# Moving one chunk's load behind four output stores on a DMA queue

## The chip, the cores and the metric

The kernel runs on one core of a Trainium2 chip. The metric is the device time of one execution in microseconds (us), given as the median of several. TensorE does the matmuls and writes their results to banks of a memory called PSUM; VectorE, ScalarE and GpSimd do the elementwise work, and SyncE issues nearly all DMAs, in program order; "the queue" below is SyncE's. In the profile they are PE (with PEld for its weight loads), DVE, ACT, POOL and SP; a q after the name (SPq, ACTq) is that engine's sequencer, which issues DMAs.

## The reference

```python
# q, k, v: (8 batches, 8 heads, 576 positions, 64)
scores = scale * (q @ k^T)
ret    = scores * Dmat            # gamma_h ** (i - j) for i >= j, else 0
attn   = ret @ v                  # retention, causal, decaying
x      = attn as (4608 tokens, 512)
h      = max(x @ w1, x @ w2, x @ w3)      # w1..w3: 512 x 768
out    = h @ w_out                        # 768 x 512
```

The kernel walks the 4608 tokens in 36 chunks of 128 positions for the attention and in 9 tiles of 512 tokens for the network, four chunks to a tile. While it computes the network of tile t, it prepares the attention of tile t + 1 and loads chunks beyond that.

## The kernel before

These are the parts that matter here, cut. A chunk from number 7 on is loaded in 34 DMAs: 16 small ones for q, 16 for a second copy of k (both laid out so that VectorE can transpose them), one each for k and v. The tiles for q and kx have two buffers, so the load of chunk 10 can't start before chunk 8's has been transposed.

```python
def load_blocks(g, *blocks):
    for n, src in (("q", q), ("kx", k)):
        if 0 in blocks:
            raws[n, g] = raw.tile([P, NP, C // 32, 32], FP32, tag=n, ..., bufs=2)
        for blk in blocks:
            for a in range(4):
                nc.sync.dma_start(raws[n, g][32 * a:32 * a + 32, :, blk, :], src[...])

def load(g):
    if g >= BY_PE and ("q", g) not in raws:
        load_blocks(g, *range(C // 32))
    ...                                     # then k and v, one DMA each (more at a batch border)
```

Tile 0 goes through a plain path, whose last step copies four outputs out of PSUM and stores them. The output tile "osb" has two buffers:

```python
opool = ctx.enter_context(tc.tile_pool(name="opool", bufs=2))
...
def downs_plain(t, h):                      # tile 0
    ps = [(ps_x, ps_y)[m % 2].tile([P, DM], ...) for m in range(4)]
    for fb in range(NF):
        for m, b in enumerate(ps):
            nc.tensor.matmul(b[:], ...)
            if fb == NF - 1:
                osb = opool.tile([P, DM], FP32, tag="osb", name="osb")
                nc.scalar.copy(osb[:], b[:])
                nc.sync.dma_start(out[t * NT + m * P:t * NT + (m + 1) * P, :], osb[:])
        yield
```

Tile 1 starts with 12 plain "up" groups for the feature blocks 2 to 5 (four matmuls, eight records in the trace, each), of which the first three take the PSUM banks ps_x[0], ps_x[1], ps_x[0] in turn, the banks of tile 0's outputs 0 and 2. From then on outputs are made by `downs`, with `total` and `store`, on the same queue and the same "osb" buffers.

The order of work is written by hand, in twelve slots to a tile (cut to tile 0's last slot and the first of the common rule):

```python
if t == 1:
    a, b, c, d = range(CPT, 2 * CPT)        # chunks 4..7, prepared during tile 0
    ...
    at(11, (values, [c, d], [d, d + 1]), (load_blocks, d + 2, 3), (load, d + 2),
       (transposes, d + 1), (load, d + 3))  # d + 3 = chunk 10
    return todo
for n in range(0, CPT, 2):
    a, b, m = CPT * t + n, CPT * t + n + 1, 6 * (n // 2)
    at(m, (keep, a), (transposes, b), (decay_values, b), (load, b + 2))
    ...
```

Of the kernel before, what the change touches and what calls it, by code (L numbers as in the profile page):

```python
# [79 lines left out]
def kernel(  # L80
# [23 lines left out]
    CPT = NT // C  # L104
# [50 lines left out]
    for r in sorted({start_of(g) for g in range(NG)} - {0, None}):  # L155
        m = masks[r] = const.tile([C, C], FP32, name=f"causal{r}")
# [553 lines left out]
    def steps(t):  # L710


        todo = [[] for _ in range(3 * CPT)]

        def at(n, *what):
            for step, *args in what:
                if step is values:
                    if args[0][0] < NG:
                        todo[n].append(partial(values, args[0], [g for g in args[1] if g < NG]))
                elif args[0] < NG:  # L720
                    todo[n].append(partial(soon, partial(step, *args)) if step is load else partial(step, *args))

        if t == 1:
            a, b, c, d = range(CPT, 2 * CPT)
            at(0, (load, b))
            at(1, (scores, a), (state, a), (keep, a))
            at(2, (transposes, b), (decay_values, b), (load, c))
            at(3, (scores, b), (load_blocks, d, 0))
            at(4, (decay_values, c), (load_blocks, d, 1, 2))
            at(5, (values, [a, b], [b, c]), (load_blocks, d, 3), (load, d))  # L730
            at(6, (keep, c), (transposes, c), (load_blocks, d + 1, 0))
            at(7, (transposes, d), (decay_values, d), (load_blocks, d + 1, 1, 2))
            at(8, (scores, c), (scores, d), (load_blocks, d + 1, 3), (load, d + 1))
            at(9, (load_blocks, d + 2, 0, 1))
            at(10, (decay_values, d + 1), (load_blocks, d + 2, 2))
            at(11, (values, [c, d], [d, d + 1]), (load_blocks, d + 2, 3), (load, d + 2),
               (transposes, d + 1), (load, d + 3))
            return todo
        for n in range(0, CPT, 2):
            a, b, m = CPT * t + n, CPT * t + n + 1, 6 * (n // 2)  # L740
            at(m, (keep, a), (transposes, b), (decay_values, b), (load, b + 2))
            at(m + 2, (scores, a), (scores, b))
            at(m + 4, (decay_values, a + 2))
            at(m + 5, (values, [a, b], [b, a + 2]), (transposes, a + 2), (load, a + 4))
        return todo

    for t in range(N // NT):
        work = ffn(t)
        for todo in steps(t + 1):
            for step in todo:  # L750
                step()
            next(work, None)
# [51 lines left out]
```

## Time and profile before

| | before |
|---|---|
| median of 3 runs (range) | 805.69 us (803.97 to 806.81) |
| span of the profiled run | 804.8 us |
| TensorE busy, idle | 774.2, 30.6 us |
| longest single idle stretch of TensorE | 18.02 us, from about 130 to 148 us |
| mean granted clock of TensorE | 0.987 |

TensorE is 96% busy, so read its idle time, not its busy time: one stretch holds well over half of it. The granted clock is the share of full speed that the throttle lets TensorE have; a dip there makes the matmuls themselves longer. The lines for both are in the prediction.

### The profile page before, as it was taken

The page shows a single profiled execution, that of the slowest core. Times are in us where ns is not written, and L with a number is a line of the kernel's source. Part 1 is how long each engine was busy: PE and PEld are TensorE (multiplying, and loading weights), DVE is VectorE, ACT ScalarE, POOL GpSimd, SP SyncE. Part 2 cuts the span into 40 slices and gives each one's busy share as a digit, 9 for nine tenths or more (in the row PEclk, how much of TensorE's full clock was granted, in tenths as well). Part 3 has the DMA queues.
Part 4 walks back from the last instruction along what each step waited for, and adds up shares of the span by engine and source line. Part 5 has one row for each costly group of instructions (what it writes and reads, how often), then busy time and mean ns, then how long its engine had stood idle before and what let it go on. Part 6 is the DMA issues. An engine that isn't in the chain of part 4 may idle for free.

```text
span 804.8 us, 14293 instructions
## 1 busy us (share of the span) xinstructions
PE 774.2 (96%) x4968; PEld 619.6 (77%) x4968; DVE 552.3 (69%) x1224; ACT 316.6 (39%) x782; POOL 100.9 (13%) x124
## 2 busy tenths in 40 slices
PE   8899994699999999999999999999999999999998
PEld 7545451246888888888888888888788888888887
DVE  3897975376868784878387928783869386847672
ACT  3664630002325441544154515450445235524651
POOL 2110000031101120101111111110102010200000
PEclk9999998799999999999999999999999999999999
DMA  9996632410332333233313432334233333201001
GB/s 217 239 213 148 183 69 35 102 34 12 58 90 50 62 58 97 47 63 57 99 25 55 78 81 47 57 60 87 57 58 55 57 91 57 40 14 40 1 0 53
DMA packets 236936, 59.31 MB, mean 74 GB/s; under 512 B 217920, under 2 KB 235584, under 8 KB 236864
## 3 DMA queue, kind: packets, MB, share of 16 engines
q1 hardware_dynamic: 236432, 58.14, 33.5%
q8 instruction: 39, 0.64, 0.3%
q14 instruction: 33, 0.27, 0.1%
q10 hardware_dynamic: 432, 0.27, 0.1%
HBM read 48.89 MB, written 9.44 MB: 72 GB/s over the span
## 4 chain that ended last, share of the span: by engine, by line
PE 89%; DMA 4%; SPq 3%; DVE 3%; issue 1%; ACT 0%; DVEq 0%; ACTq 0%
PE a L579 16%; PE b L579 14%; PE up L600 13%; PE dx L424 9%; PE c L579 7%; PE d L579 5%; PE e L579 4%; PE s L240 4%; PE o L296 4%; PE dz L424 4%; PE dy L424 3%; DMA out_dram<-osb 2%; DVE s L344 2%; PE o L309 2%; PE kv L260 2%; PE down L589 2%
## 5 line engine op out<-in xcount | busy, mean ns | idle before, releaser
L559 DVE TENSOR_TENSOR part<-part 128x256 f32<-128x256 f32 x440 | 197.5, 457 | 61.6 <-ACT part L564 54.6
L564 ACT COPY part<-b 128x256 f32<-128x256 f32 x220 | 81.9, 372 | 151.0 <-PE b L579 137.1
L600 PE MATMUL up<-xT,w 128*128 128x512 f32 x240 | 107.7, 605 | 18.5 <-ACT osb L593 18.0
L564 ACT COPY part<-a 128x256 f32<-128x256 f32 x264 | 98.2, 372 | 53.6 <-PE a L579 43.5
L600 PEld LDWEIGHTS up<-xT,w 128*128 128x128 f32 x240 | 45.6, 193 | 74.4 <-issue 52.1
L579 PE MATMUL b<-s,n 128*128 128x256 f32 x264 | 78.8, 380 | 1.8 <-DVE s L344 1.8
L579 PE MATMUL a<-s,w 128*128 128x256 f32 x264 | 78.5, 379 | 0.0
L211 POOL TENSOR_TENSOR vd<-vraw,gk 128x512 f32<-128x512 f32 x36 | 38.5, 1070 | 228.4 <-DMA vraw<-in_v_dram 177.6
L441 DVE TENSOR_TENSOR osb<-dx,part 128x256 f32<-128x256 f32 x16 | 6.1, 419 | 77.3 <-PE dx L424 70.7
L579 PEld LDWEIGHTS b<-s,n 128*128 128x128 f32 x264 | 49.8, 190 | 9.9 <-ACT part L564 3.3
L579 PEld LDWEIGHTS a<-s,w 128*128 128x128 f32 x264 | 50.2, 190 | 6.8
L579 PE MATMUL c<-xT,w 128*128 128x256 f32 x176 | 54.2, 390 | 0.0
L579 PE MATMUL b<-xT,n 128*128 128x256 f32 x176 | 52.4, 379 | 0.0
L579 PE MATMUL d<-s,w 128*128 128x256 f32 x176 | 52.4, 379 | 0.0
L579 PE MATMUL e<-xT,w 128*128 128x256 f32 x176 | 45.2, 379 | 0.0
L579 PE MATMUL a<-xT,n 128*128 128x256 f32 x176 | 45.2, 379 | 0.0
L424 PE MATMUL dx<-To,H 128*128 128x256 f32 x192 | 44.8, 383 | 0.0
L559 DVE TENSOR_TENSOR h<-part 128x256 f32<-128x256 f32 x88 | 37.4, 425 | 6.3
L424 PEld LDWEIGHTS dx<-To,H 128*128 128x128 f32 x192 | 35.9, 190 | 5.7 <-issue 1.0
L240 PEld LDWEIGHTS s<-qT,kT 64*128 64x128 f32 x576 | 33.7, 188 | 8.1 <-PE b L579 4.0
L402 POOL TENSOR_TENSOR H<-h,H 128x256 f32<-128x256 f32 x24 | 18.2, 759 | 171.9 <-DVE H L401 89.6
L603 DVE TENSOR_TENSOR h<-h,up 128x512 f32<-128x512 f32 x20 | 13.7, 684 | 36.6 <-PE up L600 36.3
(104 smaller groups left out, 1296.1 us busy)
## 6 DMA issues: line engine op xcount, KB each, us to landing
bits<-in_moe_w_dram SPq DMA_DIRECT2D x36, 256.0 KB, 5.1
out_dram<-osb SPq DMA_DIRECT2D x35, 256.0 KB, 2.3
kraw<-in_k_dram SPq DMA_DIRECT2D x32, 256.0 KB, 3.0
vraw<-in_v_dram SPq DMA_DIRECT2D x32, 256.0 KB, 3.4
qraw<-in_q_dram SPq DMA_DIRECT2D x464, 16.0 KB, 1.8
kxraw<-in_k_dram SPq DMA_DIRECT2D x464, 16.0 KB, 1.8
bits<-in_moe_w_out_dram SPq DMA_DIRECT2D x6, 512.0 KB, 5.2
qraw<-in_q_dram SPq DMA_DIRECT2D x6, 256.0 KB, 4.4
```

Source lines behind the costliest of these rows:

```text
L211: nc.gpsimd.tensor_tensor(t[:], raws.pop(("v", g))[:], gk[:].unsqueeze(2).to_broadcast([C, H, D]), op=ALU.mult)
L240: nc.tensor.matmul(s[j][:, p, :], lhsT=kT[r, p, :], rhs=qT[r, p, :], start=True, stop=True)
L260: nc.tensor.matmul(kvs[g][half(h % 2), h // 2, :], lhsT=kr[r:, h, :], rhs=vds[g][r:, h, :], start=True, stop=True)
L296: nc.tensor.matmul(o[n % 2][half(c), m, n // 2, :], lhsT=vds[g][:, h, :], rhs=sts[g][:, h % 2, h // 2, :], start=m == 0 and n < 2, stop=be ...
L309: nc.tensor.matmul(o[n % 2][half(c), m, n // 2, :old], lhsT=states[g][r, h // 2, :], rhs=qks[g]["q"][r, h // 2, :old], start=False, stop=True,
L344: nc.vector.tensor_tensor(dst, a, b, op=ALU.add if sign == "+" else ALU.subtract)
L402: urgent.append(lambda: (pool(s3, a11, a21, op=ALU.subtract), pool(s4, a12, s2, op=ALU.subtract)))
L424: nc.tensor.matmul(out[m], lhsT=hS[n](fp)[:, m * P:(m + 1) * P], rhs=late["T"][n][:, fp, :], start=first and fp == 0 and (m == 0 or last a ...
L559: nc.vector.tensor_tensor(out, a, b, op=op)
L564: nc.scalar.copy(t[:], ps[step[0]][:])
L579: nc.tensor.matmul(ps[chain][:], lhsT=factor(w, fb), rhs=xS[t][x], start=n == 1, stop=ends, skip_group_check=True)
L600: nc.tensor.matmul(ps[:], lhsT=w_sb[i, fb][:, dc * P:(dc + 1) * P], rhs=xT[t][:, dc, :], start=(dc == 0), stop=(dc == NDC - 1))
```

## The change

The intent is to get tile 0's stores out as soon as their data are ready: chunk 10's load leaves the last slot of tile 0 and becomes the first load of the next tile's first slot, which is emitted after the stores.

```diff
             at(11, (values, [c, d], [d, d + 1]), (load_blocks, d + 2, 3), (load, d + 2),
-               (transposes, d + 1), (load, d + 3))
+               (transposes, d + 1))
             return todo
         for n in range(0, CPT, 2):
             a, b, m = CPT * t + n, CPT * t + n + 1, 6 * (n // 2)
-            at(m, (keep, a), (transposes, b), (decay_values, b), (load, b + 2))
+            at(m, (keep, a), (transposes, b), (decay_values, b))
+            if a == 2 * CPT:
+                at(m, (load, a + 2))
+            at(m, (load, b + 2))
```

## The prediction

> **What bounds the kernel now.** I began with the busy shares and the clock strip of the page, then read what stands just before TensorE's one large idle stretch, then followed that stretch back through the waits and the order of ScalarE, of the DMA queue and of VectorE. The page first:
>
> ```profile
> PE 774.2 (96%) x4968; PEld 619.6 (77%) x4968; DVE 552.3 (69%) x1224; ACT 316.6 (39%) x782; POOL 100.9 (13%) x124
> PEclk9999998799999999999999999999999999999999
> L600 PE MATMUL up<-xT,w 128*128 128x512 f32 x240 | 107.7, 605 | 18.5 <-ACT osb L593 18.0
> ```
>
> TensorE is busy for 774.2 of 804.8 us, so all its idle time is 30.6 us, and 18.0 of that stands in one place: ahead of an "up" matmul, released by the copy of a finished output from PSUM (line 593). The clock strip has a dip in the same place, slices 6 and 7 (120.7 to 161.0 us). The waits of 120 to 150 us, TensorE's and ScalarE's, and the queue's of 95 to 200 us, name the links:
>
> ```profile
> PE up L600 <- ACT osb L593: 18.0, 1, 18.0
> ACT osb L593 <- DMA out_dram<-osb: 21.9, 1, 21.9
> SPq L195 <- DVE qT L184: 8.1, 1, 8.1
> ```
>
> TensorE waits for a copy, the copy waits for a store to land (the output tile "osb" has two buffers and tile 0 makes four outputs), and a load on the store's queue waits 8.1 us for a transpose. The timelines of TensorE, ScalarE and the queue put times to this (start us, length us):
>
> ```profile
> 126.52 3.60 PE L600 MATMUL up<-xT,w 128*128 128x512 f32 x8
> 148.13 4.46 PE L600 MATMUL up<-xT,w 128*128 128x512 f32 x5 [18.02 <-ACT osb L593]
> ...
> 124.14 0.59 ACT L593 COPY osb<-down 128x512 f32<-128x512 f32 x1 [11.24 <-PE down L589]
> 125.00 0.58 ACT L593 COPY osb<-down 128x512 f32<-128x512 f32 x1 [0.27 <-PE down L589]
> 147.49 1.23 ACT L593 COPY osb<-down 128x512 f32<-128x512 f32 x2 [21.90 <-DMA out_dram<-osb]
> ...
> 118.92 0.50 SPq L207 DMA_DIRECT2D vraw<-in_v_dram  x1
> 127.61 7.64 SPq L195 DMA_DIRECT2D qraw<-in_q_dram  x16
> 135.29 7.54 SPq L195 DMA_DIRECT2D kxraw<-in_k_dram  x16
> 142.88 0.43 SPq L207 DMA_DIRECT2D kraw<-in_k_dram  x1
> 143.41 0.53 SPq L207 DMA_DIRECT2D vraw<-in_v_dram  x1
> 144.04 5.04 SPq L594 DMA_DIRECT2D out_dram<-osb  x4
> 149.17 7.55 SPq L195 DMA_DIRECT2D qraw<-in_q_dram  x16
> ```
>
> The first output is ready at 124.14 + 0.59 = 124.73. Its store stands in the queue behind the 34 DMAs of chunk 10's load, which can't begin before 127.6, when chunk 8's q buffer has been transposed, and then take 16.4 us to issue. So the store goes out at 144.04, 19.3 us after its data were ready. The third copy follows at 147.49, and only its end (148.1) frees the PSUM bank that the second "up" group of tile 1 wants.
>
> **What the Trainium skill says.** "DMA: Bandwidth & Descriptors", section "Anatomy of one DMA", says that DMA engines wait on no semaphore: a wait is served by the issuing sequencer before it dispatches. So a waiting load holds up the stores queued behind it; the trace agrees (no issue between 119.4 and 127.6 us, though a store was ready at 124.73). The same section gives about 50 ns for a sequencer's dispatch; here an issue takes 7.64 / 16 = 0.48 us, and I use that. "TensorE: Matmul & The Clock Gate", section "Part 1: The HAM clock gate", has the clock at half rate after an idle window of some 3.4 us and back at full rate after about as long a busy one. The stretches view agrees (columns: stretch, length, busy us of TensorE, weight loads, VectorE, ScalarE, GpSimd, granted clock, DMA share, GB/s):
>
> ```profile
> 130.20:148.00 17.80, 0.00 (x0) 0.00 (x0) 0.89 (x3) 0.51 (x1) 0.00 (x0) 0.64 0.38 86
> 148.00:151.00 3.00, 2.87 (x4) 1.32 (x5) 0.00 (x0) 1.15 (x3) 0.00 (x0) 0.50 0.53 186
> 151.00:154.00 3.00, 3.00 (x7) 1.28 (x6) 0.01 (x1) 0.00 (x0) 0.00 (x0) 0.78 0.22 33
> 154.00:157.00 3.00, 3.00 (x8) 1.33 (x7) 2.90 (x7) 0.00 (x0) 0.00 (x0) 1.00 0.24 36
> ```
>
> **The change, part by part.** It adds and removes no instruction. The order of the built programs is the same on TensorE, VectorE, ScalarE and GpSimd; on the DMA queue alone the four stores of tile 0 now stand before chunk 10's 16 + 16 + 1 + 1 DMAs, and chunk 11's load follows as before.
>
> Stores: the first can issue at about 124.8, when the queue is idle. From issue to landing the four stores of before took 2.0 to 3.4 us, median 2.6. It lands between 127.4 and 128.2, the third copy (0.59 us) ends by 128.0 to 128.9, the fourth 0.6 us later. TensorE wants that PSUM bank at 126.52 + 3.60 = 130.12. So the wait of 18.02 us should vanish whole, with 1.2 to 2.1 us to spare. The first "up" group's own copy to h comes after those four on ScalarE, but not before 130.1 in any case.
>
> Clock: after the stall, 24 records of "up" matmuls took 12.62 us (the chain's piece at 148.13). At full clock 16 take 7.06 us (its pieces at 71.76 and 186.95), so 24 take 10.59. Without the idle stretch this 2.03 us goes too.
>
> VectorE is no new limit here: by 131.13 it has done all that it did before the stall, and next needs the second "up" group, at 130.12 + 3.53 = 133.65. In the kernel before it sat idle 22.86 us at this point, and from 154 us on, where the clock is full, TensorE had no pause; that stretch repeats itself earlier.
>
> Sum: 18.02 + 2.03 = 20.05 us, all on the path that sets the end, since the TensorE work after it (96% busy to the end) simply starts that much earlier. 805.69 - 20.05 = 785.64, which I round to 785.7.
>
> **The rivals.** First, the loads come too late, and their wait takes the place of the one removed. The queue is done with the stores at about 130; chunk 10's load then issues until 130 + 16.4 = 146.4 instead of 144.0, while its users move up 20 us. Its last piece, v, lands 3.4 us after its issue (the page's median), so at about 149.3; GpSimd's scaling of it stood at 172.72, so is now due at 152.7. Its transposes stood at 192.83 and are due at 172.8. It holds, by 3.4 us at the closest. Chunk 11's load took 17.0 us (149.17 to 166.12) and ends at about 163.4, its v landing near 166.3. Its scaling stood at 184.70 and is due at 164.65: 1.6 us late. But GpSimd's next instruction stood at 195.16 (now 175.1), and the attention matmuls that read this v stood at 223.8 (now 203.8). So it is absorbed, and the queue, which waited 27.9 us for a transpose before chunk 12's load at 194.15, catches up there. If I am wrong, TensorE idles for some 2 to 5 us in tile 1: 788 to 791.
>
> Second, the store still lands too late, say beyond 4.7 us, or the third copy waits for something else too. Then a pause of one to three microseconds stays, with little or no lost clock if it is below the 3.4 us window: 786.5 to 789. Speaking against it: the store goes out onto nearly idle DMA engines, where in the kernel before it followed two 256 KB loads and still took only 3.4.
>
> Third, the gain is given back later, by waits that were hidden: in tiles 3 to 6 the chain of waits also passes through a store (3.5 to 4.8 us each) ahead of VectorE's sums, and TensorE idles up to 1.5 us per 80 us stretch. Those stand 250 us later, in stages that this change shifts as a whole, since the queue is back in step by 174. I give it 1 us at most.
>
> **Range and chances.** The three runs of before span 2.8 us, so their median is good to about 1 us; the gain itself I hold good to 1.5 us, with a tail upwards from the first two rivals. That makes 784.0 to 788.0. The line of 2% is 805.69 x 0.98 = 789.6, 3.9 us above my figure; only a wait of more than 4 us in tile 1 would cross it. So faster 0.95, within 2% 0.045, slower 0.005, since no instruction was added.
>
> **What would show it.** Right: the first store issues near 124.8 and copies 3 and 4 lie before 130; the "up" group shows no idle of 18 us; the clock strip has no dip in slices 6 and 7; scores follow at 140.7 instead of 160.75; TensorE's idle time in all is about 12.5 us; chunk 10's load issues from about 130 to 146. Wrong: a new idle stretch of TensorE between 130 and 220 released by a DMA, GpSimd or a transpose; or the dip in the clock stays although the idle stretch is gone.

## The result, and the profile after

The changed kernel took 785.23 us (median of 4 runs, 782.70 to 786.94), against 805.92 us for the kernel before (4 runs, 803.97 to 806.81): ratio 0.9744, 95% interval 0.9712 to 0.9776. A ratio is the mean time of one kernel's fast runs over the mean of the other's fast runs of the same rounds, so it is not quite the ratio of the medians quoted.

From the page of the changed kernel, the busy shares, the clock strip and the group of the "up" matmuls:

```profile
PE 770.4 (99%) x4968; PEld 618.3 (79%) x4968; DVE 551.8 (71%) x1224; ACT 316.9 (41%) x782; POOL 100.4 (13%) x124
PEclk9999999999999999999999999999999999999999
L600 PE MATMUL up<-xT,w 128*128 128x512 f32 x240 | 105.4, 595 | 0.5 <-DVE xT L184 0.5
```

Idle before the "up" matmuls fell from 18.5 to 0.5 us, their mean from 605 to 595 ns, and the strip has no dip. TensorE idles 780.9 - 770.4 = 10.5 us in all. Now the timelines of the changed kernel for the same stretch, TensorE, then ScalarE, then the queue:

```profile
124.73 13.90 PE L600 MATMUL up<-xT,w 128*128 128x512 f32 x32
138.56 2.06 PE L240 MATMUL s<-qT,kT 64*128 64x128 f32 x32
...
122.36 0.58 ACT L593 COPY osb<-down 128x512 f32<-128x512 f32 x1 [11.28 <-PE down L589]
123.22 0.59 ACT L593 COPY osb<-down 128x512 f32<-128x512 f32 x1 [0.27 <-PE down L589]
125.15 0.58 ACT L593 COPY osb<-down 128x512 f32<-128x512 f32 x1 [1.35 <-DMA out_dram<-osb]
126.27 0.58 ACT L593 COPY osb<-down 128x512 f32<-128x512 f32 x1 [0.53 <-DMA out_dram<-osb]
...
122.97 4.24 SPq L594 DMA_DIRECT2D out_dram<-osb  x4
127.30 7.52 SPq L195 DMA_DIRECT2D qraw<-in_q_dram  x16
134.87 8.51 SPq L195 DMA_DIRECT2D kxraw<-in_k_dram  x16
```

The first copy ends at 122.94 and its store issues at 122.97. The third copy waits 1.35 us for a store instead of 21.90, and the 32 "up" records that were cut in two run through in one piece.

This trace is 1.79 us ahead of the other one when tile 1 begins (124.73 against 126.52 us); that lead is there at the first "up" matmul of tile 0 already (27.65 against 29.44), before anything that was changed, so it isn't the change's. I therefore compare stretches. From the first "up" matmul of tile 1 to the scores of chunk 8 it is 160.68 - 126.52 = 34.16 us before and 138.56 - 124.73 = 13.83 after: 20.33 us gained there. From those scores to the end it is 644.12 us before and 642.34 after, 1.78 us less (spans are read to 0.1 us, so this is good to about 0.1); most of that is traced below.

### The profile page after: what moved, and what is told of

Same layout as the page of the kernel before. It is cut to its first block, busy times and chain, and to the rows that moved or that the text cites. A ratio compares the mean times of both kernels' runs of the same rounds, so it can differ in the third digit from the quotient of the medians.

```text
span 780.9 us, 14294 instructions
## 1 busy us (share of the span) xinstructions
PE 770.4 (99%) x4968; PEld 618.3 (79%) x4968; DVE 551.8 (71%) x1224; ACT 316.9 (41%) x782; POOL 100.4 (13%) x124
## 4 chain that ended last, share of the span: by engine, by line
PE 95%; DVE 2%; DMA 2%; SPq 0%; issue 0%; POOL 0%; ACT 0%; DVEq 0%; POOLq 0%
PE a L579 17%; PE b L579 14%; PE up L600 13%; PE dx L424 10%; PE c L579 8%; PE d L579 5%; PE e L579 5%; PE dz L424 5%; PE s L240 4%; PE o L296 4%; PE down L589 3%; PE dy L424 3%; PE kv L260 2%; PE o L309 2%; DMA out_dram<-osb 1%; DVE s L344 1%
## 5 line engine op out<-in xcount | busy, mean ns | idle before, releaser
L600 PE MATMUL up<-xT,w 128*128 128x512 f32 x240 | 105.4, 595 | 0.5 <-DVE xT L184 0.5
L472 ACT COPY osb<-dx 128x256 f32<-128x256 f32 x16 | 5.3, 375 | 84.2 <-PE dx L424 72.4
```

Of the source, the lines that this page charges most:

```text
L600: nc.tensor.matmul(ps[:], lhsT=w_sb[i, fb][:, dc * P:(dc + 1) * P], rhs=xT[t][:, dc, :], start=(dc == 0), stop=(dc == NDC - 1))
```

## The experiments

My theory: TensorE waited for a copy, the copy for a store, and the store for the 34 DMAs ahead of it, and the idle stretch then cost 2 us of clock on top. Rivals: that moving the load itself brought the gain; that the wait for chunk 8's transpose, not the issuing, was what held the store; that the slow matmuls after the stall had another cause than the clock.

**Four outputs without a wait.** The kernel before, with the third and fourth output put into two tiles that are unused until tile 1:

```diff
-                    osb = opool.tile([P, DM], FP32, tag="osb", name="osb")
-                    nc.scalar.copy(osb[:], b[:])
+                    if m < 2:
+                        osb = opool.tile([P, DM], FP32, tag="osb", name="osb")[:]
+                    else:
+                        osb = late["S"][m - 1][:, 0:2, :].rearrange("p a f -> p (a f)")
+                    nc.scalar.copy(osb, b[:])
```

(`late["S"]` is also allocated earlier, before tile 0's outputs. Simply giving "osb" four buffers didn't build: the pool allocated after it needed 56 KB a partition and 52.97 were left.)

> The kernel before with its queue order unchanged, but tile 0's third and fourth outputs copied into two other, still unused tiles, so that no copy waits for a store. Theory (TensorE waits for a copy, the copy for a store, the store for 34 DMAs ahead of it on the queue): cutting the chain at the copy is as good as cutting it at the queue. Stores still issue at about 144, yet the third copy comes by 128, the idle stretch of 18 us is gone, time 785.5 (784 to 788). Rival (the gain comes from moving chunk 10's load itself out of 127 to 144 us): nothing gained, 805 to 807.

Measured: 786.35 us (4 runs), ratio 0.9744 (0.9715 to 0.9772). The queue's timeline of this run, and TensorE's:

```profile
128.58 7.63 SPq L195 DMA_DIRECT2D qraw<-in_q_dram  x16
...
145.80 1.00 SPq L597 DMA_DIRECT2D out_dram<-osb  x2
...
127.49 13.90 PE L603 MATMUL up<-xT,w 128*128 128x512 f32 x32
```

The load starts 1.09 us after tile 1's first matmul, exactly as in the kernel before (127.61 - 126.52), and the first store issues at 145.80, as late as ever. Yet TensorE runs through. So the load's time is not the cause; the copies' wait is.

**Tile 0's stores on another queue.** The kernel before, with `nc.scalar.dma_start` for the four stores.

```diff
-                    nc.sync.dma_start(out[t * NT + m * P:t * NT + (m + 1) * P, :], osb[:])
+                    nc.scalar.dma_start(out[t * NT + m * P:t * NT + (m + 1) * P, :], osb[:])
```

> The kernel before with tile 0's four stores issued from ScalarE's queue, the loads untouched. Theory: stores issue at about 125, 126, 128 and 129, third copy by 129, no idle stretch of TensorE, 785.5 (784 to 788), the same as the change although chunk 10's load still issues from 127.6 to 144. Rival (it is the load's time that counts): 805 to 807.

Measured: 785.51 us (4 runs), ratio 0.9742 (0.9700 to 0.9784). The time is as expected, but this run doesn't separate the load's time as cleanly as I meant. The loads didn't stay untouched: chunk 10's issued from 132.10 instead of 127.61, because a load of chunk 9 waited for a store on the other queue (the queue's waits, 110 to 170 us):

```profile
SPq L195 <- DMA out_dram<-osb: 8.8, 1, 8.8
```

In the traces every DMA of these two queues takes one of eight semaphores (the counters that tell of a landing) in turn, and an issue waits until the previous user of its semaphore has landed: the load here issued at 128.67, when the store before it on the same semaphore landed at 128.65. The clean answer is that of the run above.

**Half, and a quarter, of the load ahead.** The changed kernel with 16, then 8, of chunk 10's 34 DMAs put back ahead of the stores. The first of the two edits (the other has block 0 alone ahead):

```diff
-               (transposes, d + 1))
+               (transposes, d + 1), (load_blocks, d + 3, 0, 1))
...
-                at(m, (load, a + 2))
+                at(m, (load_blocks, a + 2, 2, 3), (load, a + 2))
```

> The changed kernel with blocks 0 and 1 of chunk 10 (16 of its 34 DMAs) put back ahead of the stores. Theory (each DMA ahead costs its 0.475 us of issue): first store at 127.6 + 16 x 0.475 = 135.2, lands 2.0 to 2.6 us later, copy done 0.7 after that, TensorE idle 7.9 to 8.4 us from 130.1 (times of the kernel before), lost clock 2.0 to 2.3 us: 10.3 us above the changed kernel, 795.5 (794 to 797.5). Rival (the wait for chunk 8's transpose is what holds the store, the issues hardly count): within 2 us of the run with 8 ahead, whichever level both take.

> The changed kernel with block 0 alone of chunk 10 (8 of its 34 DMAs) put back ahead of the stores. Theory: first store at 127.6 + 8 x 0.475 = 131.4, copy done at 134.1 to 134.7, TensorE idle 4.0 to 4.6 us, lost clock 0 to 2.3 us as the idle stretch is only just longer than a clock window: 785.2 + 4.3 + 1.2 = 790.7 (789 to 792.5). Rival (all or nothing with the wait): the same as with 16 ahead.

Measured: 796.95 us with 16 ahead (4 runs; ratio 0.9876, 0.9843 to 0.9909) and 794.40 us with 8 ahead (4 runs; 0.9845, 0.9806 to 0.9885). The first is in its range; the second is 1.9 us above its own. The medians are 2.55 us apart and the intervals overlap, so the times alone don't exclude the rival's "within 2 us". TensorE's timelines do, 16 ahead first:

```profile
138.37 12.48 PE L600 MATMUL up<-xT,w 128*128 128x512 f32 x24 [8.03 <-ACT osb L593]
```
```profile
137.76 13.50 PE L600 MATMUL up<-xT,w 128*128 128x512 f32 x24 [4.45 <-ACT osb L593]
```

The stalls are 8.03 and 4.45 us, as worked out (7.9 to 8.4 and 4.0 to 4.6): they follow the number of DMAs ahead, with 18.02 for all 34. So the issuing counts, and the rival falls. What I had mis-sized, by this trace, is the clock. The 24 records after the stall take 10.57 us at full clock (next run), so they lost 1.91 us after a stall of 8.03 and 2.93 us after one of only 4.45, more than after 18.02 us (12.62 - 10.57 = 2.05). The stretches view of the run with 8 ahead (columns as in the prediction) shows the dip:

```profile
134.00:138.00 4.00, 0.24 (x1) 0.24 (x2) 0.33 (x1) 0.76 (x2) 0.00 (x0) 0.86 0.45 148
138.00:142.00 4.00, 4.00 (x5) 1.61 (x6) 0.00 (x0) 0.90 (x2) 0.00 (x0) 0.50 0.47 151
142.00:146.00 4.00, 4.00 (x9) 1.67 (x8) 1.46 (x4) 0.00 (x0) 0.00 (x0) 0.79 0.22 33
```

The clock was halved 0.88 us before work came back, and stayed low for the first 5.95 us of it: the same view, cut finer, shows 0.50 from 136.88 to 143.71 us. It shows 0.50 from 135.22 to 152.29 in the kernel before and from 135.42 to 142.25 with 16 ahead, which is 4.16 and 3.88 us beyond the return of work. Each loss (2.93, 2.05, 1.91) is about half of that time, whatever the length of the stall. The Trainium skill, "TensorE: Matmul & The Clock Gate", section "Part 1: The HAM clock gate", says that the windows run freely, so the place of the change in the work varies; that a short stall here cost more clock than a long one fits with it. But this is one trace each, and the profiled run with 8 ahead was the slowest of its four (797.72 us; the others 791.76 to 794.65) at the lowest granted clock (0.989; the others 0.993 to 0.998). It was at 0.50 from 24.3 to 34.4 us in its start-up, too, and starts tile 1 late for that. By an estimate from its mean of 0.998, the run of 791.76 us lost about 0.002 x 790 = 1.6 us of clock in all, so 2.93 is not what 8 ahead always costs.

**A stall kept busy.** The kernel before, with 20 matmuls into a bank that nobody reads, put between the first and the second "up" group of tile 1. Its output is still right.

```diff
         for i in range(3):
+            if fb == 2 and i == 1:
+                ps = ps_r.tile([P, NT], FP32, tag="r", name="busy")
+                for _ in range(20):
+                    nc.tensor.matmul(ps[:], lhsT=ident[:], rhs=xT[t][:, 0, :], start=True, stop=True)
             up_plain(t, h, fb, i)()
```

> The kernel before with 20 idle-filling matmuls (128x512, into a PSUM bank nobody reads) after the first up group of tile 1: TensorE computes nothing useful but stays busy for about 17.3 of the 18 us. Theory (about 2 us of the gain is clock): the stall's length stays, its clock dip goes, the 24 records after it take 10.4 instead of 12.6 us, time 805.9 - 2.2 = 803.7 (802.5 to 805). Rival (slow records after the stall have another cause, such as the DMA traffic of 148 to 151 us): no gain, 805.9, records still slow.

Measured: 803.70 us (6 runs, before 805.79), ratio 0.9978 (0.9948 to 1.0008), so by time alone a gain of 2.1 us that the interval doesn't quite tell from nothing. The timelines do, the kernel before first, then this run:

```profile
148.13 12.62 PE L600 MATMUL up<-xT,w 128*128 128x512 f32 x24 [18.02 <-ACT osb L593]
```
```profile
129.90 17.33 PE L665 MATMUL busy<-xT,ident 128*128 128x512 f32 x40
148.34 10.57 PE L600 MATMUL up<-xT,w 128*128 128x512 f32 x24 [1.11 <-ACT osb L593]
```

The useful work resumes as late as before (148.34 against 148.13), at full clock: 10.57 us where it was 12.62. The granted clock of every run of this kernel was 0.998 to 1.000; that of the kernel before was 0.981 to 0.989. The slow records were the clock's, and 2.05 us is their size.

**A short stall kept busy.** The run with 8 ahead, with four such matmuls (the edit is the same, with `range(4)`).

> The run with 8 DMAs ahead, which came out above its range (794.4, expected 789 to 792.5; its profile has a stall of 4.4 us as worked out, but 13.5 us for the 24 records after it where 10.4 is full speed), with four idle-filling matmuls (3.5 us) in that stall. Theory (the missing 3 us are the clock, which dips after 4 us of idleness as far as after 18): stall 4.4, records at full speed, 785.2 + 4.4 = 789.6 (788.5 to 791.5). Rival (the load split in two costs more in another way): 793 to 795.

Measured: 791.69 us (5 runs, before 807.17 on that chip), ratio 0.9796 (0.9771 to 0.9820); 0.9796 of 805.9 is 789.5. The median lies 0.2 us above the expected range, the ratio in the middle of it. The 24 records took 10.57 us again:

```profile
135.00 10.57 PE L600 MATMUL up<-xT,w 128*128 128x512 f32 x24 [0.81 <-ACT osb L593]
```

The stretch from the first "up" matmul to the scores took 18.33 us instead of 21.48. That is 4.50 more than without a stall (13.83), which the stall of 4.45 us explains. So in the traces the missing 3 us were the clock, and the split load cost nothing besides its stall. The intervals of the two ratios overlap, so the times alone don't show it.

**Chunk 11 first.** The changed kernel with `(load, b + 2)` put ahead of `(load, a + 2)`, which makes chunk 10's load 17 us later.

> The changed kernel with chunk 11's load ahead of chunk 10's, which makes chunk 10 some 17 us later: its v issues near 160.4 instead of 143.95, lands near 163.4, is scaled by 164.6. Theory (chunk 10's load has 3 to 4 us of slack at v and over 15 elsewhere): only the state matmuls of chunk 10, due at 163.7, wait, about 1 us: 786.2 (785 to 788). Rival (the loads are nearly on the path and the change only just got away with it): 5 us or more, 790 and up.

Measured: 787.53 us (5 runs), ratio 0.9767 (0.9740 to 0.9794), in range, beside 783.69 us and 0.9716 for the changed kernel in the same call. TensorE's waits have one new line, of the expected size:

```profile
PE kv L260 <- POOL vd L211: 1.2, 1, 1.2
```

Against the changed kernel's trace, chunk 10's v was issued 16.4 us later after the start of tile 1 and scaled 13.3 us later, so its scaling had 3.1 us of slack, where the prediction had 3.4. TensorE, which reads that v later still, waited only 1.2 us. The medians differ by 3.8 us and this wait is 1.2; the rest I can't place, since the one trace has nothing else new.

**The changed kernel again.**

> The changed kernel once more, for comparison on the same chip with the runs beside it: ratio 0.974 (0.972 to 0.977), about 785.

Measured: 783.69 us (5 runs, before 805.79), ratio 0.9716 (0.9688 to 0.9743), just below the expected 0.972 to 0.977.

**Later stores on another queue.** The same wait in small may remain at the later tiles. In the first trace of the changed kernel TensorE's waits after the start-up are these:

```profile
PE b L579 <- DVE s L344: 1.0, 2, 0.7
...
PE a L579 <- ACT osb L472: 0.5, 1, 0.5
```

There VectorE waits for an "osb" buffer whose store stands behind a load (four times in that trace, 6.0 us in all), and its sums come late. So I put the stores of tiles 1 to 7 on ScalarE's queue, twice, and once on GpSimd's:

```diff
-            nc.sync.dma_start(block.rearrange(...)[:, blocks], osb[:, blocks])
+            (nc.sync if last else nc.scalar).dma_start(block.rearrange(...)[:, blocks], osb[:, blocks])
```

> The changed kernel with the stores of tiles 1 to 7 (not the last tile) on ScalarE's queue. Theory (the same head-of-queue wait remains in small at the later tiles, where TensorE waits 1.0 us for VectorE's sums and 0.5 us for the copy of line 472 in all): at most 1.5 us better, 784 (783 to 785.5). Rival (ScalarE's sequencer is held up by the waits for VectorE and by the issues, and delays its copies): 786 to 792.

> The changed kernel with the stores of tiles 1 to 7 on ScalarE's queue once more: its ratio to before was 0.970, the changed kernel's of the same call 0.9716, with overlapping intervals. If the removed waits (1.7 us of TensorE's) are the gain, the ratio is 0.969 to 0.971 again, 781 to 782.5; if it was chance, 0.9725 to 0.975.

> The changed kernel with the stores of tiles 1 to 7 on GpSimd's queue, an engine that is 13% busy. Theory: the same gain as on ScalarE's queue if issuing is cheap there, 781.5 (780 to 783.5). Rival (issuing from GpSimd takes so long, or so disturbs VectorE, that sums and scalings come late): 786 to 800.

Measured: 780.97 us (6 runs, ratio 0.9700, 0.9670 to 0.9730), then 782.95 us (4 runs, 0.9692, 0.9674 to 0.9710); on GpSimd's queue 782.23 us (4 runs, 0.9690, 0.9669 to 0.9712). The first is 2.0 us below its range: I had expected at most 1.5 us of gain. The second's ratio is in its range and its median 0.45 us above; the third is in its range.

**All stores of tiles 0 to 7 on ScalarE's queue, loads in their old order.** This is the kernel before with the two diffs that use ScalarE's queue.

> The kernel before, all loads in their old order, with the stores of every tile but the last on ScalarE's queue. Theory (all that matters is that a store stands behind no load): as good as the change and the later stores together, 781.5 (780 to 784). Rival (loads that share semaphores with stores of another queue are held up, 8.8 us in the run with tile 0's stores there, and something then starves): 786 or more.

Measured: 782.02 us (4 runs), ratio 0.9684 (0.9667 to 0.9702). A load waited 12.8 us for the landing of a store, by the shared semaphores, and TensorE did not stall for it (13.83 us in the table below).

The intervals of the changed kernel and of these overlap, so the times alone don't settle the small gain. The traces say more. This table has, for each, when tile 1's first "up" matmul starts, how long it is from there to the scores of chunk 8, from there to the end of the span, and what TensorE waits for in that last part (the lines for VectorE's sums, for the copy of line 472 and, with chunk 11 first, for the scaled v). All are in us; "to the end" is good to about 0.1:

| kernel | tile 1 starts | to the scores | to the end | waits |
|---|---|---|---|---|
| before | 126.52 | 34.16 | 644.12 | 2.7 |
| before, stall kept busy | 126.47 | 32.37 | 647.96 | 5.0 |
| 16 ahead | 126.75 | 24.03 | 644.12 | 2.3 |
| 8 ahead | 129.72 | 21.48 | 644.70 | 2.8 |
| 8 ahead, kept busy | 127.17 | 18.33 | 646.80 | 3.8 |
| changed, first trace | 124.73 | 13.83 | 642.34 | 1.5 |
| changed, second trace | 127.01 | 13.83 | 642.56 | 1.7 |
| chunk 11 first | 125.61 | 13.82 | 643.87 | 2.7 |
| before, four outputs | 127.49 | 13.82 | 643.99 | 2.5 |
| before, tile 0's stores on ScalarE's queue | 125.64 | 13.83 | 643.73 | 2.5 |
| changed, later stores on ScalarE's | 124.26 | 13.83 | 640.11 | 0 |
| the same again | 125.86 | 13.82 | 640.32 | 0 |
| changed, later stores on GpSimd's | 125.78 | 13.82 | 640.40 | 0 |
| before, all on ScalarE's | 126.00 | 13.83 | 640.17 | 0 |

Three things can be read from it. Every kernel that keeps TensorE from stalling has 13.82 or 13.83 us in the middle column, whatever way it does so. In the last part, the kernels whose later stores stand behind loads need 642.3 to 648.0 us and the four others 640.1 to 640.4, so these versions beat the changed kernel too, by some 2 us in this part. The listed waits (1.5 us in its first trace) are about two thirds of that; the rest lies in TensorE's own busy time there (637.4 us, against 636.6 with all stores on ScalarE's queue), and its cause was not looked for. And the spread of single runs is in the start (124.3 to 129.7) and in those late waits, neither of which the change touches.

## Why the prediction was right

The range (784.0 to 788.0) held the result, and the kernel is faster by more than 2%, as forecast. Step by step:

- **The wait of 18.02 us goes whole.** It did. The first store issued at 122.97, which is 124.76 on the other trace's clock; predicted 124.8. The stores landed in 2.0 to 2.3 us, where I had allowed 2.0 to 3.4, so the third copy ended 2.6 us before the bank was wanted (125.73 against 124.73 + 3.60), where I had predicted 1.2 to 2.1.
- **2.03 us of clock.** The run with a busy stall puts it at 2.05.
- **The sum, 20.05.** The stretch gained 20.33 us, in both traces of the changed kernel. Of the missing 0.28, 0.17 is how I took the stall: from the modelled end of the last matmul, 3.60 us after the first "up", while the filling matmuls show that the next one could have started 3.43 us after it (129.90 - 126.47). The rest is not placed.
- **First rival, late loads.** It didn't come. Chunk 10's v was scaled at 150.61, directly behind the GpSimd instruction before it. Chunk 11's came at 163.93, 25.37 us after the scores instead of 24.02: 1.35 us late, predicted 1.6. GpSimd's next instruction stood 34.48 us after the scores in both kernels, so it was absorbed.
- **Second rival, a rest of the stall.** Ruled out by the trace. My remark there, that a pause would cost little clock if it is below the window, wasn't tested; what was tested, 4.45 us, cost more clock in its trace than the long stall did.
- **Third rival, a gain given back later.** It wasn't: the last part was 1.78 us shorter in the first trace. That is not the change's doing as far as the traces tell. The late waits differ from run to run, and they were 2.7 us in the one trace of before and 1.5 in this one. They are the same head-of-queue wait, which I had named but left alone.
- **Idle time of 12.5 us.** It was 10.5: 1.2 us of the difference are these late waits, the rest, 0.8, is a luckier start-up (5.5 us idle instead of 6.4).

## What to carry to other kernels

Read a DMA queue like an engine: what stands at its head, what it waits for, and which ready transfer is stuck behind it. A store that gives back a buffer wanted soon should stand behind no load that waits for a buffer and isn't needed for long; changing the order, two more output tiles or another issuing engine cut the same chain equally well here. When a single long wait goes, look also for the clock: the matmuls after it got shorter too here, by 2.05 us.

## What the Trainium skill lacked or had wrong

- "DMA: Bandwidth & Descriptors" gives about 50 ns for a sequencer's dispatch in its section "Anatomy of one DMA", but for a DMA issued from GpSimd. For an issue on SyncE's or ScalarE's queue the page has no time measured on trn2, only a vendor's cycle count for earlier generations, set against trn3's. Here one issue of 16 KB on SyncE's queue took 7.64 / 16 = 0.48 us, and 34 DMAs 16.4 us.
- The same page, section "Issuing engines are not separate DMA queues", says that issuing from several engines saves only the sequencer's time, usually small relative to the DMA. Here the saved time was also that spent waiting at the head of the queue: the kernel before with all stores but the last tile's on ScalarE's queue took 0.9684 of the time that it takes without.
- No page that I read says that a DMA on one queue can be held by one on another, through the program's shared semaphores: 8.8 and 12.8 us in the two runs with tile 0's stores on ScalarE's queue.
- "TensorE: Matmul & The Clock Gate", section "Part 1: The HAM clock gate", is right in kind (0.50 granted from 148 to 151 us after the stall, 1.00 from 154 on). It reckons the cost as the throttled time times the missing share of the clock. That holds here only for the part of it with work: in the kernel before the clock was at half for 17.07 us (135.22 to 152.29), 4.16 of them after work came back, and 2.05 us were lost. By the length of the stall it gives no cost; here it was 2.05 us after 18.02 us of idleness, 1.91 after 8.03 and 2.93 after 4.45, one trace each.
